# A bias table built in SBUF from SBUF by shifted row reads, and due times for ScalarE's and VectorE's work

## The chip, the cores and the metric

One core of a Trainium2 chip. The metric is the device time of one launch, in microseconds (us), as the median of several launches. Runs are compared only with runs of the kernel before on the same chip and in the fast state. Units of the profile are us unless ns is said.

## The reference, cut to what matters

```python
# q, k, v: (8 batches, 8 heads, 576 positions, 64); bias_table: (32 buckets, 8 heads)
scores = q @ k.T / 8 + bias_table[bucket(|i - j|)]     # bias depends on the distance alone, per head
x = softmax(scores) @ v                                # -> (4608 tokens, 512)
h = maximum(x @ w_in, 0.0)                             # w_in: 512 x 2048
return h * h @ w_out                                   # w_out: 2048 x 512
```

Because the bias depends only on the distance i - j, exp(bias) of one head is one row of numbers, and row p of its table is that row shifted by p. The kernel multiplies the exponentials with this table ("the band") in place of adding the bias to the scores. Beyond a certain distance the bias is constant and falls out, so the table is only 384 wide.

## The kernel before

One TensorE matmul makes the eight rows of exp(bias): `tv_sb`, 8 partitions x 512. To get the shifted copies the kernel writes them to DRAM and reads them back with overlapping rows:

```python
written = pool(tdram.ap(), tv_sb, 0.1, [tv])                 # SBUF -> DRAM, 8 KB; pool() issues on GpSimd
def table_read(h0, n):                                       # 4 heads in one DMA, row p shifted by p
    return pool(tb_sb[:, h0 : h0 + n, :],
        bass.AP(tensor=tdram, offset=512 * h0 + 1, ap=[[1, 128], [512, n], [1, 384]]), 0.3 * n, [written])
def table_mixed(e):                                          # table of the last block of keys, two heads mixed
    return pool(tm_sb[ds(64 * e, 64), :, :],
        bass.AP(tensor=tdram, offset=512 * e + 193, ap=[[1, 64], [1024, 4], [1, 192]]), 0.4, [written])
```

The work is cut into 96 units: a batch, a third of the queries (192), a pair of heads. A unit has scores `st` (TensorE), exponentials `et` (ScalarE), bands `et*tb_sb` (VectorE), products with the values `pv` (TensorE), and normalising `x_sb` (ScalarE and VectorE). Layer 1 is `hps`, layer 2 is `yps`.

Every operation goes through a planner at build time. It holds estimates (`occ`: time on the engine, `lat`: time until its result is there), advances each engine and takes from its waiting operations the one that can start first, or within a small allowance the one with the earliest due time. **What it fixes is the order of each engine's instructions. On the chip each engine then runs them in exactly that order and waits wherever a result is not there yet** (below, VectorE stands 15.39 us before one copy). An estimate that is too low therefore puts an instruction too early, and all that stands behind it on its engine waits with it.

```python
at, _, q = min((h for h in heads if h[0] <= first + wait), key=lambda h: (h[2][0].due, h[0], h[1]))
o.at, o.done = at, at + o.lat
if o.load:
    dma = max(dma, at + 1.35) + o.load
    o.done = dma + 1.15
```

## Time and profile before

| | before |
|---|---|
| median (lowest to highest) | 429.52 us (429.16 to 429.67) |
| span of the profiled run | 428.8 us |
| TensorE busy in 10-20, 20-30, 30-40 us | 9.88, 6.68, 8.05 |
| first scores, first bands, first values (`pv`), second unit's values | 9.47, 17.38, 18.28, 21.25 us |

The tenths of busy time, the stretches and the first 40 us are printed in the prediction. Two lines are added here, from the DMA view cut to the stretch from 6 to 40 us (what moves, issuing queue, count, size of one, median us from issue to landing). They are the measure for how fast the loads of keys and queries are served while the table is on its way:

```profile
kh<-in_k_dram POOLq DMA_DIRECT2D x5, 144.0 KB, 7.4
qh<-in_q_dram POOLq DMA_DIRECT2D x5, 144.0 KB, 7.5
```

### The profile page before, as it was taken

The numbers are of one execution on the slowest core, as the hardware profiler recorded it, in microseconds if no ns is written. First come the engines' busy times: TensorE is split into PE (matmuls) and PEld (weight loads), VectorE is DVE, ScalarE is ACT, GpSimd is POOL, SyncE is SP. The second block draws the span as 40 slices with busy tenths as digits, with TensorE's granted clock in tenths as the row PEclk, the third lists the DMA queues.
The fourth block names the chain that finished last, engine by engine and source line by source line (L and its number), as shares of the span: only waits on it lengthen the run. The fifth ranks groups of instructions, "written<-read, shape, count | busy, mean of one in ns | idle before, by whom it ended". The sixth has DMA issues, their size and how long they took to land.

```text
span 428.8 us, 9401 instructions
## 1 busy us (share of the span) xinstructions
PE 407.6 (95%) x3604; PEld 261.0 (61%) x3604; DVE 314.6 (73%) x939; ACT 299.1 (70%) x584; POOL 132.5 (31%) x179
## 2 busy tenths in 40 slices
PE   6968799999999998998999999999999999999996
PEld 3556587765676665665666666666666666666552
DVE  5778988757687767876867876877867876867761
ACT  2779668876888786786787787787787787784000
POOL 6874828605800192005800094004100000000000
PEclk9989999999999999999999999999999999999999
DMA  8999999959993499077991599056402300000011
GB/s 104 144 186 178 132 152 102 101 97 137 104 95 65 93 92 143 28 98 94 90 97 53 92 85 149 28 95 95 52 27 55 79 26 26 26 26 26 24 50 73
DMA packets 164717, 36.66 MB, mean 85 GB/s; under 512 B 152600, under 2 KB 159872, under 8 KB 164672
## 3 DMA queue, kind: packets, MB, share of 16 engines
q0 software_dynamic: 130048, 19.46, 58.6%
q1 hardware_dynamic: 34624, 16.60, 15.5%
q8 instruction: 28, 0.46, 0.5%
q14 instruction: 17, 0.14, 0.1%
HBM read 37.75 MB, written 16.52 MB: 127 GB/s over the span
## 4 chain that ended last, share of the span: by engine, by line
PE 81%; DVE 7%; ACT 5%; DMA 4%; issue 1%; SPq 0%; POOL 0%; POOLq 0%
PE yps L931 28%; PE hps L855 25%; PE pv L727 15%; PE st L603 7%; PE pv L701 3%; ACT et L629 3%; DMA kt<-k 2%; PE st L578 2%; DVE y L944 2%; DMA kh<-in_k_dram 1%; ACT r L769 1%; DVE x_sb L780 1%; DVE rt L874 1%; DVE et L647 1%; ACT r L799 1%
## 5 line engine op out<-in xcount | busy, mean ns | idle before, releaser
L629 ACT ACTIVATE et<-st 128x960 f16<-128x960 f32 x192 | 167.7, 882 | 60.1 <-PE st L603 59.8
L855 PE MATMUL hps<-x_sb,w_in_sb 128*128 128x384 f16 (+1 forms) x896 | 154.9, 303 | 3.2 <-DVE rt L874 1.9
L931 PE MATMUL yps<-w_out_sb,g_sb 128*128 128x512 f16 x576 | 152.0, 379 | 3.4 <-DVE y L944 2.7
L855 PEld LDWEIGHTS <-w_in_sb 128*128 128x128 f16 x896 | 83.2, 98 | 56.2 <-issue 5.6
L647 DVE TENSOR_TENSOR et<-et,tb_sb 128x384 f16<-128x384 f16 (+2 forms) x288 | 78.0, 310 | 35.6 <-ACT et L629 32.4
L234 POOL DMA_DIRECT2D vz<-in_v_dram x80 | 57.9, 743 | 135.7 <-PE pv L727 73.5
L727 PE MATMUL pv<-et,vz 128*128 128x192 f16 x804 | 86.4, 250 | 5.1 <-DVE x_sb L780 4.7
L780 DVE TENSOR_TENSOR x_sb<-pv,r 64x192 f16<-64x192 f32 x192 | 67.8, 353 | 25.8 <-ACT r L799 22.7
L931 PEld LDWEIGHTS <-g_sb 128*128 128x128 f16 x576 | 55.6, 98 | 48.7 <-issue 5.5
L727 PEld LDWEIGHTS <-vz 128*128 128x128 f16 x804 | 63.4, 99 | 20.4 <-issue 16.7
L870 DVE TENSOR_TENSOR g_sb<-rt 128x384 f16<-128x384 f16 x192 | 67.1, 355 | 5.6 <-ACT rt L866 1.4
L769 ACT ACTIVATE r<-pv 64x192 f32<-64x192 f32 x192 | 62.4, 325 | 12.3 <-PE pv L727 7.8
L866 ACT ACTIVATE rt<-hps 128x384 f16<-128x384 f32 x100 | 48.4, 486 | 27.4 <-PE hps L855 26.6
L874 DVE TENSOR_SCALAR rt<-hps 128x384 f16<-128x384 f32 x92 | 51.3, 557 | 10.9 <-PE hps L855 7.2
L603 PE MATMUL st<-qt,kt 64*128 64x192 f16 x768 | 51.3, 250 | 0.0
L234 POOL DMA_DIRECT2D k<-in_k_dram x48 | 31.0, 683 | 25.9 <-DMA q<-in_q_dram 13.6
L799 ACT ACTIVATE r<-r 128x192 f32<-128x192 f32 x96 | 34.8, 363 | 3.0
L603 PEld LDWEIGHTS <-kt 64*128 64x128 f16 x768 | 31.9, 95 | 3.6 <-issue 1.6
L944 DVE TENSOR_SCALAR y<-yps 128x512 f32<-128x512 f32 x36 | 24.8, 690 | 9.2 <-PE yps L931 8.4
L578 PEld LDWEIGHTS <-km_sb 128*128 128x128 f16 x192 | 18.6, 100 | 15.3 <-issue 0.6
L578 PE MATMUL st<-qt,km_sb 128*128 128x96 f16 x192 | 24.5, 211 | 0.1
L234 POOL DMA_DIRECT2D q<-in_q_dram x18 | 24.6, 1398 | 0.0
(32 smaller groups left out, 116.6 us busy)
## 6 DMA issues: line engine op xcount, KB each, us to landing
out_dram<-y SPq DMA_DIRECT2D x36, 256.0 KB, 2.3
vz<-in_v_dram POOLq DMA_DIRECT2D x64, 64.0 KB, 3.2
q<-in_q_dram POOLq DMA_DIRECT2D x18, 192.0 KB, 8.0
k<-in_k_dram POOLq DMA_DIRECT2D x48, 72.0 KB, 7.1
w_in_sb<-in_moe_w_in_dram POOLq DMA_DIRECT2D x4, 512.0 KB, 9.3
w_out_sb<-in_moe_w_out_dram POOLq DMA_DIRECT2D x4, 512.0 KB, 10.0
kh<-in_k_dram POOLq DMA_DIRECT2D x8, 144.0 KB, 6.7
qh<-in_q_dram POOLq DMA_DIRECT2D x8, 144.0 KB, 6.9
```

The source lines that it names most:

```text
L234: return lambda: io(eng.dma_start(out=out_, in_=in_))
L578: nc.tensor.matmul(st[:, g, 2 * IC : 2 * IC + IC // 2], km_sb[:, p % KB, :], qts[p][:, ds(c0 + g * IC // 2, IC // 2)], start=True, stop=True,)
L603: nc.tensor.matmul(st[:, e, ds(i * IC, IC)], kts[p][rows, ts(2 * g + i, 128)], qts[p][rows, ds(c0, IC)], start=True, stop=True,)
L629: io(nc.scalar.activation(out=et, in_=sts[n, g][:, :, 0:w], func=EXPF, scale=SCALE))
L647: nc.vector.tensor_tensor(out=sl, in0=sl, in1=tb_sb[:, 2 * hp : 2 * hp + 2, ds(w0, w)], op=MULT)
L727: nc.tensor.matmul(pv if jt < 4 else pv.rearrange("p (g c) -> p g c", g=2), vz[:, jt, 2 * hp + e, :], ets[n, jt // 2][:, e, ds(jt % 2 * IC ...
L769: nc.scalar.activation(out=rs[n][o : o + 64, :], in_=pvt[n, e][64 - o : 128 - o, 0:IC], func=LNF)
L780: nc.vector.tensor_tensor(out=x_sb[o : o + 64, hp, ds(ring(blk), IC)][:, ::-1], in0=pvt[n, e][o : o + 64, 0:IC], in1=rs[n][o : o + 64, :], ...
L855: nc.tensor.matmul(hps[:, ds(i * w, w)], w_in_sb[:, kk, ts(nt, 128)], x_sb[:, kk, ds(o, w)], start=(kk == 0), stop=(kk == 3),)
L870: io(nc.vector.tensor_tensor(out=g_sb[:, ts(u, k), o : o + w], in0=rt, in1=rt, op=MULT))
L874: io(nc.vector.tensor_scalar_max(out=rt, in0=hpt[blks, u][:, 0 : 2 * IC], scalar1=0.0))
L931: nc.tensor.matmul(ypt[j], g_sb[:, nt, ds(128 * m % RING, 128)], w_out_sb[:, nt, :], start=(nt == 0), stop=(nt == 15),)
```

## The change

The intent: no round trip through DRAM, fewer DMAs in GpSimd's queue, and the mixed table made by VectorE from the finished tables. Besides this the planner's load estimates are raised, and the work of ScalarE and VectorE for layer 1, transposes and key copies gets due times in place of first come, first served. The core of the diff:

```diff
-                o.done = dma + 1.15
+                o.done = dma + 1.9                        # planner: loads land later
-                0.48 * n,
+                0.6 * n,                                  # ... and take longer
-    written = pool(tdram.ap(), tv_sb, 0.1, [tv])
-    def table_read(h0, n): ...                            # 2 DMAs of 4 heads, from DRAM, GpSimd
-    def table_mixed(e): ...                               # 2 DMAs, from DRAM, GpSimd
+    def table(h):                                         # 8 DMAs of one head, from SBUF, SyncE
+        row = bass.AP(tensor=tv_sb.tensor, offset=512 * h + 1, ap=[[512, 1], [1, 128], [1, 384]])
+        return add("SP", "set", 0.45, 4.5, dma(nc.sync, tb_sb[:, h, :], row), [tv])
+    tbs = [table(h) for h in range(H)]
+    def table_mixed(e):                                   # VectorE; needs the tables of four heads
+        rows = ds(64 * e, 64)
+        src = tb_sb[rows, e::2, ds(192 - 64 * e, 192)]
+        return add("DVE", "tm", 0.4, 0.5, lambda: io(nc.vector.tensor_copy(out=tm_sb[rows, :, :], in_=src)),
+            [x[e] for x in tbs], T0 + P * 6)
...
-                [loads_qk[b, 2 * hp][w], id_in],
+                [loads_qk[b, 2 * hp][w], id_in, *(kq_ready[0] if p == 1 else [])],
...                                                        # due times: ev (transposes out of PSUM), km (key copies), turn (transposing loads)
-            r = Op("ACT", 0.41, 0.55, relu, [m, ...], LATE)
+            r = Op("ACT", 0.41, 0.55, relu, [m, ...], m.due)      # same for the two squares on VectorE
```

Note the source of each table DMA: 128 reads of 768 bytes, all from **one** partition of SBUF, each one element further. The plan counts on 4.5 us from issue to landing for every one of the eight.

> **What bounds the kernel now.** I read the page first, then busy time in stretches of 10 us, then the timeline of the first 40 us with the waits there, and last the chain of waits.
>
> ```profile
> PE   6968799999999998998999999999999999999996
> ACT  2779668876888786786787787787787787784000
> DMA  8999999959993499077991599056402300000011
> ...
> 10.00:20.00 10.00, 9.88 (x107) 5.76 (x103) 7.04 (x23) 7.01 (x9) 8.22 (x12) 1.00 0.97 135
> 20.00:30.00 10.00, 6.68 (x81) 5.28 (x81) 6.89 (x23) 7.44 (x16) 7.15 (x12) 0.84 1.34 182
> 30.00:40.00 10.00, 8.05 (x113) 6.16 (x111) 8.14 (x28) 9.71 (x19) 6.20 (x9) 0.99 1.33 200
> 40.00:50.00 10.00, 8.79 (x124) 6.66 (x123) 9.47 (x31) 8.57 (x19) 7.79 (x10) 1.00 1.24 111
> ...
> 240.00:250.00 10.00, 10.00 (x80) 6.06 (x79) 8.29 (x27) 8.12 (x18) 2.95 (x5) 1.00 0.54 96
> ```
>
> In the stretches (PE, PEld, DVE, ACT, POOL busy, then granted clock, DMA share, GB/s) TensorE is busy 10.00 of 10 us from about 100 us to 420 us, with gaps of 1 to 1.5 us only at 160-170 and 190-210. The starts of the scores (two matmuls from km_sb per unit of work, 96 units) come at 242.13 us for unit 60 and 382.30 us for unit 95: 140.17 / 35 = 4.0 us a unit, against 2.67 us of ScalarE work per unit (exponentials 1.65, two logarithms 0.67, reciprocal 0.36). So the long middle is TensorE's and no reordering on ScalarE or VectorE can shorten it much. The first 100 us are different: TensorE is busy 86 of them, some of that on warm-up matmuls that do nothing. That stage is what can be had.
>
> ```profile
> 5.61 0.68 DVE L383 CAST tv_sb<-tvp 8x512 f16<-8x512 f32 x1 [0.24 <-PE tvp L378]
> 6.58 0.54 POOL L234 DMA_DIRECT2D t_bias<-tv_sb  x1 [1.33 <-DVE tv_sb L383]
> 7.11 2.79 POOL L234 DMA_DIRECT2D vz<-in_v_dram  x4
> 8.90 0.45 PE L465 MATMUL tp<-id_sb,kh 96*64 96x96 f16 x6 [1.71 <-DMA kh<-in_k_dram]
> 9.47 0.37 PE L578 MATMUL st<-qt,km_sb 128*128 128x96 f16 x2
> 10.31 3.48 ACT L629 ACTIVATE et<-st 128x960 f16<-128x960 f32 x4 [2.54 <-PE st L603]
> 11.78 0.77 POOL L234 DMA_DIRECT2D tb_sb<-t_bias  x1 [1.89 <-DMA t_bias<-tv_sb]
> 15.29 0.80 POOL L234 DMA_DIRECT2D tb_sb<-t_bias  x1
> 17.38 2.71 DVE L647 TENSOR_TENSOR et<-et,tb_sb 128x384 f16<-128x384 f16 x12
> 18.28 1.78 PE L727 MATMUL pv<-et,vz 128*128 128x192 f16 x10
> 19.00 1.33 POOL L234 DMA_DIRECT2D tm_sb<-t_bias  x2
> 20.24 0.84 POOL L234 DMA_DIRECT2D w_in_sb<-in_moe_w_in_dram  x1
> 38.13 0.83 PE L855 MATMUL hps<-x_sb,w_in_sb 128*128 128x192 f16 x8
> ...
> tb_sb<-t_bias POOLq DMA_DIRECT2D x2, 384.0 KB, 4.9
> tm_sb<-t_bias POOLq DMA_DIRECT2D x2, 96.0 KB, 4.1
> ```
>
> The first exponential is done at about 11.3 us (10.31 + 0.98), yet the first band multiplication with the table runs at 17.38, and twelve of them come in one burst: they had piled up behind the table. The table existed in SBUF at 6.29 (5.61 + 0.68), so 11 us went into writing it to DRAM and reading it back. Values (pv) begin at 18.28. With four buffers for the exponentials, ScalarE cannot start unit 5 before that, and it idles 3.0 us in 10-20 and 2.6 us in 20-30. In 30-40 it is the bound with 9.71 busy. Layer 1 starts at 38.13, when the first block is normalised; only then has TensorE filling work.
>
> [...]GpSimd sat 1.89 us on the t_bias write, with the loads behind it in its queue. [...]the transposing load kt from SyncE lands in 2.8 us at the median, and in 6.74 us at 159 us while GpSimd's queue is full. [...]The new source rows are partitions 0 to 7. [...]I therefore take the 4.0 us per unit, not the 95%, as what TensorE needs.
>
> **The change part by part.**
>
> 1. GpSimd's queue. Five DMAs go: issue 0.54 + 0.77 + 0.80 + 1.33 = 3.44 us, and the waits 1.33 (for tv_sb) and 1.89 (for t_bias), 6.66 us in all. The loads behind start earlier: the first values at 5.25 instead of 7.11, pair 3 of keys and queries at about 9.5 instead of 13.99, the first w_in at about 13.8 instead of 20.24. Their bytes leave that queue too: 2 x 384 + 2 x 96 KB = 0.98 MB, at the 182 GB/s of 20-30 worth 5.4 us. The issue gain and the byte gain are the same gain seen twice, not a sum: loads from w_in on come some 5 to 6 us earlier if they get the engines.
>
> 2. The table itself. Eight SyncE DMAs of 96 KB, issued from about 6.3 us at 0.42 us each (SyncE's small loads take 0.40 to 0.43). [...]each lands in the 2.4 to 2.8 us of those small loads plus a little: pair 0 by about 10, all by about 14. [...]Two DVE copies are added (under 0.5 us each, VectorE 70% busy there): nothing.
>
> 3. Unit 0's scores. Pair 1's transposes now come after pair 0's evacuation, and the planner expects loads later (1.9 for 1.15, 0.6 for 0.48), which is nearer to the trace: the first kh is in use at 5.50, the old constants say 4.7, the new ones 5.7. Before, TensorE stood 1.71 us in front of pair 1's keys while pair 0 was ready (qt finished at 7.78). Scores go from 9.47 to about 7.9: 1.5 us, all of it on the path, as ScalarE waited for them.
>
> 4. Due times for layer 1's evacuation, evacuation of transposes, bands. In the middle TensorE always has work, so nothing. In 40-70, where TensorE idles 1.2 + 1.5 + 0.7 us and hps waits on rt for 1.9 us in the whole trace, earlier evacuation frees banks: about 0.5 us gained, of uncertain sign, because the same order delays exponentials on a full ScalarE.
>
> The sum on ScalarE's path: its idle time from 10 to 30 is 5.5 us, plus 1.5 us from part 3: 7.0 us if ScalarE never waited again. It will not be perfect: each unit still runs values, logarithms, reciprocal, products in a loop through two banks, and this loop takes 2.3 to 3.4 us a unit (pv at 21.25, 24.64, 26.89, 29.83, 32.48), about as long as ScalarE's own 2.67. I take 60%, 4.2 us, with part 4 inside the noise. TensorE is full afterwards, so this carries through to the end: 429.5 - 4.2 = 425.3 us.
>
> **The rivals.**
>
> A. [...]All 128 descriptors of a head read one SBUF row[...]. Then pairs 2 and 3 arrive[...] instead of about 21, VectorE (in order) stands before their bands, and values of units 5 and 6 slip from 29.83 and 32.48[...]. [...]Against it: [...]later loads are still early. It would make 428 to 433 us.
>
> B. The transfers are the bound. The DMA share is above 1 from 15 to 90 us, and 0.77 MB are only moved to the hardware queue, interleaving with the same q, k, v loads. Then only 0.2 MB are really gone and the loads for the second batch come hardly earlier. For it: shares of 1.2 to 2.0. Against it: in 10-15 the engines idled (101 GB/s) because of the bounce. It would make 426.5 to 428.
>
> C. All of the startup shifts, second batch and weights too, by the full 7 us, and the stalls at 160 and 190-210 (2.8 us) go as the order changes: 420 to 422. The stalls come from a late transposing load under a full queue, which the change does not address, so this is unlikely.
>
> **Range and chances.** I weigh the main path at 55% (424 to 426.5), A at 22%, B at 13%, C at 7%, and 3% for something worse, such as table reads blocking the engines for the q, k, v loads. That gives 425.3 us and a range of 421.8 to 430.5. Two per cent are 8.6 us: more than ScalarE's whole idle time in 10-30 with part 3, so faster by over 2% gets 0.06; slower needs the start to slip by as much, 0.04.
>
> **What the new profile would show.** Right: scores of unit 0 near 8 us, the first band before 12, first values by 13, w_in issued near 14, first hps near 31 to 34, ScalarE above 8.5 of 10 in 10-20 and 20-30, the 4.0 us per unit unchanged. Wrong in the way of A: tb_sb landing times that grow head by head[...], VectorE waiting for tb_sb. Wrong in the way of B: kh and vz landing later from issue than now, PE waiting for kh. Wrong in part 4: the spacing of units in the middle above 4.0 us, or new waits of pv for bands or of st for exponentials.

The forecast came to 429.5 - 4.2 = 425.3 us, in a range of 421.8 to 430.5. Where the text above is marked as cut, it said of the hardware what no trace or run of this case shows: how transfers wait and share, how places in SBUF are served (with a rate for such reads, and the landing times and reasons of rival A that came from it), and why the 4.0 us per unit were taken in place of the busy share. No term of the 425.3 is cut. The 428 to 433 us of A, which counted for 22% in the range, rested on the cut rate and can't be followed from what is left.

## The result, and the profile after

| | before | after |
|---|---|---|
| median (lowest to highest) of 4 runs | 429.57 (429.16 to 429.67) | 452.44 (452.05 to 453.37) |
| ratio | 1 | 1.0537, 95% interval 1.0519 to 1.0556 |

All eight runs of this table were fast. Ratios here and below are the mean time of one kernel's fast runs over the mean of the other's of the same rounds, so not quite the ratio of the medians. The verdict "same" means within 2%, "unclear" that the interval reaches across the 2% line. The change made the kernel 5.4% slower; the predicted range ended at 430.5.

The page of the kernel after: TensorE by 40 slices of 11.25 us, its granted clock, and the chain of work that ended last by engine.

```profile
PE   7415688999979999899999999999999999999996
...
PEclk9965999999999999999999999999999999999999
...
PE 70%; DVE 11%; DMA 8%; SPq 5%; ACT 2%; issue 2%; DVEq 0%
```

Where TensorE had 6, 9, 6, 8 in its first slices it now has 7, 4, 1, 5. From the eighth slice on the two rows are alike: a difference of the start that is carried to the end. SyncE's issue (SPq) and transfers (DMA) stand in the chain with 13%, where the kernel before had 4% of transfers and nothing of SyncE; the table's issues and transfers are 4% and 3% of it, the transposing loads of keys 5%. The unit starts say the same: the 60th unit starts its scores at 261.2 us (before: 242.1), the 95th at 398.2 (382.3); between them (398.2 - 261.2) / 35 = 3.9 us a unit, no slower than the 4.0 of before. At the 95th unit the new kernel is 15.9 us late and at the end of the span 21.2 (450.0 - 428.8); where the last 5.3 us come from was not looked into.

The first 40 us in stretches (busy time of PE, PEld, DVE, ACT, POOL, then granted clock, DMA share, GB/s), and the lines of the timeline that tell why:

```profile
10.00:20.00 10.00, 3.86 (x52) 2.55 (x50) 3.17 (x13) 3.00 (x4) 3.71 (x6) 1.00 1.04 61
20.00:30.00 10.00, 4.32 (x46) 2.90 (x44) 1.15 (x4) 3.54 (x6) 4.67 (x7) 0.84 1.30 119
30.00:40.00 10.00, 0.76 (x6) 0.70 (x6) 2.62 (x9) 0.00 (x0) 3.25 (x5) 0.50 1.13 151
```

```profile
6.37 22.98 SPq L233 DMA_DIRECT2D tb_sb<-tv_sb  x8
...
18.03 1.16 DVE L649 TENSOR_TENSOR et<-et,tb_sb 128x384 f16<-128x384 f16 x5 [6.43 <-DMA tb_sb<-tv_sb]
...
36.54 0.35 DVE L401 COPY tm_sb<-tb_sb 64x768 f16<-64x768 f16 x1 [15.39 <-DMA tb_sb<-tv_sb]
...
39.24 1.76 PE L729 MATMUL pv<-et,vz 128*128 128x192 f16 x10 [14.91 <-DVE x_sb L782]
```

Read the last block from the top. The eight issues keep SyncE 22.98 us (0.56 to 5.5 us each), where 8 x 0.42 = 3.4 us had been counted on: it looks as if SyncE is held while earlier transfers are undone, which was not shown. The first bands run at 18.03 after a wait of 6.43. At 36.54 comes the key line: VectorE's next instruction is the copy into the mixed table, it needs the seventh table, and VectorE stands before it for 15.39 us. The normalising of unit 0 (`x_sb`) stands behind it on VectorE, so the second unit's `pv` on TensorE wait 14.91 us, ScalarE has nothing to do (0.00 in 30-40), and the granted clock shows 0.50 in the same stretch, in which TensorE is busy 0.76 of 10 us.

The same DMA view of 6 to 40 us as shown of before:

```profile
tb_sb<-tv_sb SPq DMA_DIRECT2D x8, 96.0 KB, 13.8
kh<-in_k_dram POOLq DMA_DIRECT2D x5, 144.0 KB, 14.4
qh<-in_q_dram POOLq DMA_DIRECT2D x5, 144.0 KB, 14.3
```

The tables take 13.8 us at the median, and loads that have nothing to do with them land after 14.4 us in place of 7.4. Two suspects, then: the tables are late and stand in front of VectorE, or the slow reads slow everything else.

### The profile page after: what moved, and what is told of

The parts are those of the page before. It is cut to its first block, busy times and chain, and to the rows that moved or that the text cites. A ratio compares the mean times of both kernels' runs of the same rounds, so it can differ in the third digit from the quotient of the medians.

```text
span 450.0 us, 9425 instructions
## 1 busy us (share of the span) xinstructions
PE 410.2 (91%) x3615; PEld 262.8 (58%) x3615; DVE 316.1 (70%) x946; ACT 298.4 (66%) x579; POOL 129.1 (29%) x174
## 3 DMA queue, kind: packets, MB, share of 16 engines
q1 hardware_dynamic: 35776, 17.38, 18.4%
## 4 chain that ended last, share of the span: by engine, by line
PE 70%; DVE 11%; DMA 8%; SPq 5%; ACT 2%; issue 2%; DVEq 0%
PE yps L933 24%; PE hps L857 22%; PE pv L729 13%; PE st L605 5%; DMA kt<-k 5%; SPq L233 4%; DMA tb_sb<-tv_sb 3%; PE pv L703 3%; DVE x_sb L782 2%; DVE rt L876 2%; DVE et L649 2%; PE st L580 2%; DVE g_sb L872 2%; DVE y L946 1%; SPq L532 1%
## 5 line engine op out<-in xcount | busy, mean ns | idle before, releaser
L857 PE MATMUL hps<-x_sb,w_in_sb 128*128 128x384 f16 (+1 forms) x896 | 152.3, 303 | 3.3 <-DVE rt L876 1.6
L933 PE MATMUL yps<-w_out_sb,g_sb 128*128 128x512 f16 x576 | 149.6, 379 | 3.6 <-DVE y L946 3.4
L782 DVE TENSOR_TENSOR x_sb<-pv,r 64x192 f16<-64x192 f32 x192 | 67.8, 353 | 24.9 <-ACT r L801 21.7
L868 ACT ACTIVATE rt<-hps 128x384 f16<-128x384 f32 x95 | 46.2, 487 | 33.9 <-PE hps L857 33.7
L876 DVE TENSOR_SCALAR rt<-hps 128x384 f16<-128x384 f32 x97 | 54.0, 557 | 11.1 <-PE hps L857 7.1
```

The source lines that it names most:

```text
L782: nc.vector.tensor_tensor(out=x_sb[o : o + 64, hp, ds(ring(blk), IC)][:, ::-1], in0=pvt[n, e][o : o + 64, 0:IC], in1=rs[n][o : o + 64, :], ...
L857: nc.tensor.matmul(hps[:, ds(i * w, w)], w_in_sb[:, kk, ts(nt, 128)], x_sb[:, kk, ds(o, w)], start=(kk == 0), stop=(kk == 3),)
L876: io(nc.vector.tensor_scalar_max(out=rt, in0=hpt[blks, u][:, 0 : 2 * IC], scalar1=0.0))
L933: nc.tensor.matmul(ypt[j], g_sb[:, nt, ds(128 * m % RING, 128)], w_out_sb[:, nt, :], start=(nt == 0), stop=(nt == 15),)
```

## The experiments

My theory was the place of the source: all reads of one table come from one partition and are served one after the other, so are those of neighbouring partitions, and the eight heads follow each other. The rivals: that many reads of one row, or SBUF to SBUF transfers as such, are slow; that the transfers in general were the bound; and that the due times or the new estimates did the damage. Where the expectations speak of this theory by a letter, it is A. Each expectation was on record before its run.

### 1. The transfer by itself

The kernel before, with transfers of 96 KB appended in the quiet tail, each kind waiting for the one before (one look, its state unknown, 536.47 us as planned by the addition; the result stays right). Not shown in the cut are a first read of the row and one of the row without the shift; this last did not wait for the read before it.

```diff
+    io(nc.sync.dma_start(out=pr["row"], in_=row(0)))              # one row, shifted
+    io(nc.sync.dma_start(out=pr["across"], in_=g_sb[:, 0, 0:384]))  # source over 128 partitions
+    io(nc.sync.dma_start(out=pr["dram"], in_=bass.AP(tensor=tdram, offset=1, ap=[[1, 128], [1, 384]])))
+    for h in range(H): io(nc.sync.dma_start(out=pr8[:, h, :], in_=row(h)))     # eight heads
+    for to, other in ((same, 1), (apart, 4)):                     # two queues, 4 + 4
+        for i in range(4):
+            io(nc.sync.dma_start(out=to[0][:, i, :], in_=row(0)))
+            io(nc.scalar.dma_start(out=to[1][:, i, :], in_=row(other)))
```

> The kernel before, with table-sized transfers (128 rows of 768 B) issued one at a time after its last output, when no other transfer runs. Theory A[...]: one head from one row takes 4 us or more[...], the same rows without the shift too, the copy whose source is spread over 128 partitions about 2 us, the rows read from DRAM about 2 to 3 us; eight heads in a row about 29 us. Two queues at once: four heads of partition 0 and four of partition 1[...] 29 us, four of partition 0 and four of partition 4[...] clearly less, 15 to 20. Theory B (the transfers are only slow because the load queue competes for the engines): one head about 2.5 us, eight about 8, no difference between sources. Theory C (one row is what is slow[...]): like A, but partitions 0 and 1 together as fast as 0 and 4.

The timeline of the tail (start, duration, and in brackets what VectorE's copy waited for, so the time of the transfer):

```profile
436.95 0.14 DVE L1024 COPY tv_sb<-pr_row 8x1 f16<-8x1 f16 x1 [5.93 <-DMA pr_row<-tv_sb]
...
442.33 0.14 DVE L1024 COPY tv_sb<-pr_across 8x1 f16<-8x1 f16 x1 [2.08 <-DMA pr_across<-g_sb]
...
447.01 20.81 SPq L1039 DMA_DIRECT2D pr_eight<-tv_sb  x8
477.61 0.14 DVE L1024 COPY tv_sb<-pr_eight 8x1 f16<-8x1 f16 x1 [30.57 <-DMA pr_eight<-tv_sb]
...
511.73 0.14 DVE L1024 COPY tv_sb<-pr_same 8x1 f16<-8x1 f16 x1 [32.58 <-DMA pr_same<-tv_sb]
...
532.17 0.14 DVE L1024 COPY tv_sb<-pr_apart 8x1 f16<-8x1 f16 x1 [18.91 <-DMA pr_apart<-tv_sb]
```

The same 96 KB land in 5.4 us (the first read) and 5.9 us from one row and in 2.0 us from 128 partitions; with the row in DRAM it took 2.9. Eight heads in a row take 30.6 us, 3.8 us a head: 98,304 B / 3.8 us = 26 GB/s. The same row read without the shift landed 8.4 us after issue, but it was queued behind another row read; from the landing of that one it took 3.1 us, so leaving out the shift does not bring it to the 2.0 of the spread source. The 29 us expected of eight heads can be had as an estimate from the kernel after: there pairs 0, 1 and 2 landed at 17.9, 25.1 and 32.9 us, 3.6 to 3.9 us a head, and 8 x 3.6 = 29. Two queues with sources on partitions 0 and 1 gain nothing (32.6 us for eight transfers); with sources on partitions 0 and 4 the same eight take 18.9. So it is neither the SBUF to SBUF transfer as such (2.0 us from 128 partitions) nor that single rows are read (18.9 us against 32.6): it counts on which partitions the rows lie. By what means was not shown. The long issue goes with it: SyncE was held 20.81 us by the eight issues here too, with nothing else running.

### 2. The table undone, and the table alone

Kernel after with the table of before; and kernel before with the table of after (both are the table hunk of the diff above, taken back and put in).

> The changed kernel with the table of before (through DRAM on GpSimd's queue), all other parts of the change kept. If the slow table is the whole loss: 427 to 430 us, since unit 0's scores come some 0.6 us earlier as in the changed kernel. If the new due times or the new transfer estimates cost something: above 433.

> The kernel before with the table part of the change alone. If the slow table is the loss: 445 to 455 us, with tb_sb landing after 7 to 17 us and VectorE held for over 10 us on tb_sb. If the loss needs the new due times: below 435.

Measured: 430.95 us without the new table (ratio 1.0017, 0.9984 to 1.005), 454.63 us with the table alone (1.0572, 1.0532 to 1.0613). The whole loss is the table's. The due times and estimates without it give nothing that can be told from zero.

### 3. The same eight transfers, with the rows in DRAM

Everything of the change stays, SyncE's eight DMAs and VectorE's copies too. Only the rows are written to DRAM first and read from there:

```diff
+    written = add("SP", "set", 0.45, 2.6, dma(nc.sync, tdram.ap(), tv_sb), [tv])
-        row = bass.AP(tensor=tv_sb.tensor, offset=512 * h + 1, ap=[[512, 1], [1, 128], [1, 384]])
+        row = bass.AP(tensor=tdram, offset=512 * h + 1, ap=[[1, 128], [1, 384]])
```

> The changed kernel, with one edit: SyncE first writes the eight rows to DRAM, and the same eight transfers read them there. Same queue, same sizes, same order. Theory A: transfers land in 3 to 5 us, all by about 16 us, VectorE does not wait for tb_sb, and the start is as I had predicted: 423 to 427 us. Theory B (competition with the loads on the same engines): landing times stay above 8 us and the time above 440.

Measured: 432.99 us (1.0058, 1.0018 to 1.0099). The timeline of this kernel:

```profile
10.52 5.07 SPq L234 DMA_DIRECT2D tb_sb<-t_bias  x8
...
16.70 2.45 DVE L652 TENSOR_TENSOR et<-et,tb_sb 128x384 f16<-128x384 f16 x10 [3.18 <-DMA tb_sb<-t_bias]
17.21 1.77 PE L732 MATMUL pv<-et,vz 128*128 128x192 f16 x10 [2.62 <-DMA vz<-in_v_dram]
```

The eight issues take 5.07 us in place of 22.98, the tables land 4.9 to 6.5 us after issue. Some 19 of the 23 us are back (452.4 - 433.0, from two chips; against before, 0.6% are left of 5.4%) with the rows in DRAM as the source: here the detour through DRAM beats the direct way. The start is now about 1 us ahead of before (first values at 17.21 in place of 18.28, where they wait 2.62 us for a load), and yet the kernel is 0.6% slower than before: that lead is lost later.

### 4. The planner told of the late tables

One-row reads as in the kernel after, but with its landing times put into the plan, so that VectorE's copy is not put too early. The figures do not all stand at their own head: by the trace, heads 0 to 7 took 6.6, 10.9, 15.3, 15.4, 17.2, 13.6, 13.3 and 14.0 us, so the plan has head 2 some 4 us too early and head 6 some 4 us too late. The same plan is used once more in section 10.

```diff
-        return add("SP", "set", 0.45, 4.5, dma(nc.sync, tb_sb[:, h, :], row), [tv])
+        occ = (0.56, 0.6, 2.1, 5.0, 4.6, 3.9, 0.6, 5.5)[h]
+        lat = (6.6, 9.7, 10.9, 15.3, 15.4, 16.3, 17.2, 13.1)[h]
+        return add("SP", "set", occ, lat, dma(nc.sync, tb_sb[:, h, :], row), [tv])
```

> The changed kernel; only the planner's figures for the eight table transfers are set to what the trace showed (issue 0.56 to 5.5 us, landing 6.6 to 17.2 us), so it places the two mixed-table copies and the bands where the tables are there. The transfers stay as slow. If the standing of VectorE in front of the mixed-table copy is most of the loss of 22 us: 433 to 440 us. If it is the slow transfers themselves, with the loads they hold up: above 445.

Measured: 449.10 us (1.0442, 1.038 to 1.0504). The long wait before the copy is gone, and only about a per cent with it. What TensorE then waited for, in 8 to 60 us (waits: us in total, times, longest):

```profile
PE tp L468 <- DMA kh<-in_k_dram: 7.9, 2, 4.5
```

The keys themselves now come late: `kh` landed 14.1 us after issue in 6 to 40 us. So a new wait had taken the old one's place, and I could not yet say which of the two was *the* loss.

### 5. The planner's new estimates alone

```diff
-                o.done = dma + 1.15
+                o.done = dma + 1.9
-                0.48 * n,
+                0.6 * n,
-                [loads_qk[b, 2 * hp][w], id_in],
+                [loads_qk[b, 2 * hp][w], id_in, *(kq_ready[0] if p == 1 else [])],
```

> The kernel before with part 3 alone: the planner's new load figures and pair 1's transposes after pair 0's evacuation; old table, old due times. My prediction said 1.5 us earlier scores carried to the end: 428. If the start is set by the loads and not by ScalarE: 429 to 431, the 0.6 to 1 us lost by the end.

Measured: 433.67 us (1.0091, 1.0024 to 1.0159): a loss of nearly a per cent (verdict: same; two of its runs took 431.4 and 431.8 us, two 435.6 and 435.9, and why is not known), where I had counted 1.5 us of gain on unit 0's scores. Unit 0's scores do start earlier (8.88 us, before 9.47), but nothing of it is left in the end.

### 6. The round trip kept, but on SyncE's queue

Kernel before; the write to DRAM and the eight reads from there on SyncE, the mixed table by VectorE's copies. No estimates or due times changed. Run again later in five rounds.

```diff
-    written = pool(tdram.ap(), tv_sb, 0.1, [tv])
+    written = add("SP", "set", 0.45, 4.4, dma(nc.sync, tdram.ap(), tv_sb), [tv])
+    def table(h):
+        row = bass.AP(tensor=tdram, offset=512 * h + 1, ap=[[1, 128], [1, 384]])
+        return add("SP", "set", 0.45, 5.5, dma(nc.sync, tb_sb[:, h, :], row), [written])
```

> The kernel before with one edit: the table goes through DRAM as before but on SyncE's queue (one write, eight reads, planned with the times that the earlier run showed: 4.4 and 5.5 us), the mixed table by two VectorE copies; GpSimd's queue is free of it. If GpSimd's queue was a bound of the start, as part 1 of the prediction has it: 425 to 428. If the transfers as such are (rival B): 428 to 432.

> The SyncE bounce again, with more rounds, to see whether its 428.9 us against 429.2 is a gain: between 0.990 and 1.002 of the kernel before.

Measured: 428.93 us (0.9984, 0.9935 to 1.0033), and again 429.29 us (0.9998, 0.9962 to 1.0034). GpSimd's queue is relieved of the table as the change intended, the first `w_in_sb` is issued at 14.29 and 14.73 us in place of 20.24, and the time is the same. That part of the expected gain is worth nothing here. Nor is the first `pv` a measure of the end in this range: they start at 21.81 in the second of these runs, 3.5 us later than before, and the time does not show it.

### 7. Two more attempts at a faster version

Run 3's kernel with measured table times in the plan and the transposing loads' due times as before; and run 6's kernel with two reads of four heads in place of eight reads.

```diff
-            add("SP", "turn", 1.25, 3.4, dmat(*x), halves[b] + [s_last.get(p - KB)], T0 + P * (first_use[p] - 2))
+            add("SP", "turn", 1.25, 3.4, dmat(*x), halves[b] + [s_last.get(p - KB)])
```

```diff
-        row = bass.AP(tensor=tdram, offset=512 * h + 1, ap=[[1, 128], [1, 384]])
+        rows = bass.AP(tensor=tdram, offset=512 * h0 + 1, ap=[[1, 128], [512, 4], [1, 384]])
```

> The run with rows from DRAM (433.0 us), with its planner told the measured times and with one part of the change taken back: the transposing loads are due at once again, not two units before their use. In that run the lead of 1.3 us of TensorE work at 100 us was gone at 120. If the later due time of these loads costs it: 427 to 430. If not: 431 to 434.

> The SyncE bounce with two reads of four heads instead of eight of one: fewer issues, the same bytes and rows. Expected equal to the eight: 427 to 430 us; below 426 it would be the best version.

Measured: 430.81 us (1.0021, 0.9976 to 1.0066) and 428.46 us (0.9966, 0.9919 to 1.0013). Neither is told from before. No version of this study clearly beats it.

### 8. Does a slow row read slow a load beside it?

In the quiet tail again: a load like that of the keys, issued from GpSimd, alone and then beside four SyncE transfers of each kind (one look, its state unknown).

```diff
+        for i in range(0 if n == "nothing" else 4):
+            io(nc.sync.dma_start(out=st4[n][:, i, :], in_=src))     # src: 128 partitions, DRAM rows, one SBUF row
+        io(nc.gpsimd.dma_start(out=ld[n], in_=k[0, 0:2].rearrange("h (p t) d -> p h (t d)", t=TPP)))
```

> The kernel before, and in its quiet tail one load of keys by GpSimd's queue (two heads, 96 rows of 1536 B each, cast to half the size), four times: with nothing beside it, beside four table-sized SyncE transfers whose source is spread over 128 partitions, beside four that read shifted rows in DRAM, beside four that read one SBUF row. If the one-row reads hold the engines up for others: alone about 3 to 4 us, beside the spread and the DRAM sources at most twice that, beside the one-row reads 10 us or more, ending nearly when they end (about 15 us). If the engines serve both queues fairly: beside one-row reads no more than beside the DRAM rows.

```profile
441.91 0.15 DVE L1040 COPY end_dram<-ld_dram 96x1 f16<-96x1 f16 x1 [6.61 <-DMA ld_dram<-in_k_dram]
...
443.31 0.63 POOL L1034 DMA_DIRECT2D ld_row<-in_k_dram  x1 [7.21 <-DVE end_row L1039]
450.16 0.15 DVE L1040 COPY end_row<-ld_row 96x1 f16<-96x1 f16 x1 [7.02 <-DMA ld_row<-in_k_dram]
...
459.89 0.16 DVE L1042 COPY end_row<-by_row 128x1 f16<-128x1 f16 x1 [2.84 <-DMA by_row<-tv_sb]
```

From issue to landing the load took 3.1 us alone, 3.8 beside sources spread over 128 partitions, 6.3 beside DRAM rows and 6.8 beside one-row reads (443.31 to 450.16, where the copy runs that waits for it). I had expected 10 us or more in the last case and missed: the load is slowed to about twice, but is not held until the row reads are through at 459.89. DRAM rows slow a load nearly as much; the comparison is not quite even, as they were issued 3.0 us before their load (432.45 and 435.48), the row reads 0.2 us before theirs. What differs is how long it goes on: the four one-row reads are under way from 443.10 to 459.89, 16.8 us, where the four of DRAM rows landed within 7.1 us of their issue. Loads that follow meet the row reads too.

### 9. Two heads only from the SBUF row

Run 6's kernel, heads 0 and 1 straight from SBUF, the other six through DRAM.

```diff
+        if h < 2:
+            row = bass.AP(tensor=tv_sb.tensor, offset=512 * h + 1, ap=[[512, 1], [1, 128], [1, 384]])
```

> The SyncE bounce (428.9 us) with the first two of eight heads read straight from their SBUF rows, as in the change, and six through DRAM. If the loss is the time in which one-row reads hold the engines (3.8 us a head, 21 us for eight): a quarter of it, 433 to 436 us. If it were mostly VectorE standing before late tables or a matter of order: 427 to 430, since unit 0's table is then early.

Measured: 430.67 us (1.0027, 0.9982 to 1.0071), a miss: the loss is not a quarter of 23 us. The two heads are there at 16.34 us, 9.6 us after the first issue, and the first bands run only at 20.81. It would fit that the length of the series costs; this run does not show it.

### 10. Late, or slowing others?

These last three were run to settle what runs 2 to 4 had left open. First the changed kernel with its eight rows on partitions 0, 4, ..., 28 in place of 0 to 7, so that no two lie closer than the 0 and 4 of run 1 (18.9 us, against 32.6 for 0 and 1):

```diff
-    tv_sb = single.tile([H, 512], FP16, name="tv_sb")
+    tv_sb = single.tile([4 * H, 512], FP16, name="tv_sb")       # the matmul writes row 4h for head h
-        row = bass.AP(tensor=tv_sb.tensor, offset=512 * h + 1, ap=[[512, 1], [1, 128], [1, 384]])
+        row = bass.AP(tensor=tv_sb.tensor, offset=512 * 4 * h + 1, ap=[[512, 1], [1, 128], [1, 384]])
```

Second, the changed kernel with its order of work untouched, but the tables come from DRAM and each pair of heads is issued only when the pair before has landed: late as after (fourth head at 24.9 and seventh at 37.5 us, after: 25.1 and 36.5), yet without reads of one row. Third, the same with the plan of run 4, which knows of the lateness.

```diff
+            if h in (2, 4, 6):   # reads a corner of the two tables before: SyncE waits here until they have landed
+                io(nc.sync.dma_start(out=late_sb[:, 2 * h : 2 * h + 2], in_=tb_sb[0:1, h - 2 : h, 0]))
-        row = bass.AP(tensor=tv_sb.tensor, offset=512 * h + 1, ap=[[512, 1], [1, 128], [1, 384]])
+        row = bass.AP(tensor=tdram, offset=512 * h + 1, ap=[[1, 128], [1, 384]])
```

> The changed kernel with the eight source rows on partitions 0, 4, ..., 28[...] in place of 0 to 7[...]. If one transfer still reads one row[...] and the transfers of the one SyncE queue go one after the other, nothing changes: 3.6 to 3.8 us a head, last table at 35 to 38 us, 449 to 454 us in all. If the 16 engines run ahead into the next transfers of the queue[...]: last table before 25 us, 430 to 442 us. I hold the first for likelier (65%).

> The changed kernel, its order of work unchanged, but the tables come from DRAM, each pair of heads issued only once the pair before has landed: late, by some 6 us a pair (about 16, 22, 28 and 33 us)[...]. If the lateness of the tables is the loss (engines in order standing before them): 445 us or more, key loads in the first 40 us landing in about 8 us. If the loss is that slow reads slow the key, query and value loads: 433 to 440 us.

> As the run before, with the planner told the late landing times of the tables as in the run that told it of them (449.1 us with one-row reads). The tables late as there, the reads not slow to others. If slowed loads make the loss of that run: 430 to 437 us. If lateness makes it: 445 us or more.

Measured: 440.38 us with the rows four partitions apart (1.0242, 1.0188 to 1.0296); 456.66 us late from DRAM (1.0605, 1.0545 to 1.0665); 439.80 us late from DRAM and told (1.0221, 1.0175 to 1.0267). The first and the last are slower than before, but whether by over 2% is unclear.

The kernel with the rows apart, whose mixed-table copy and second unit of values answer to the 36.54 and 39.24 of after:

```profile
25.64 0.35 DVE L402 COPY tm_sb<-tb_sb 64x768 f16<-64x768 f16 x1 [8.71 <-issue]
...
28.87 1.76 PE L730 MATMUL pv<-et,vz 128*128 128x192 f16 x10 [8.62 <-DVE x_sb L783]
```

I held "no change" for likelier, and it fell: with nothing altered but the partitions of the source (and, to fill them, one memset and a wider small matmul), tables 0 to 6 are there by 25.6 us in place of 36.5, and half of the loss is gone. So the place of the source rows counts inside the kernel too. From the first issue at 6.3 us the seven tables took 19.3 us, 2.8 each, where the series of run 1 took 3.8: it would fit transfers of one queue that overlap in part when their rows lie apart. That, and what limits it, was not shown.

The kernel with late tables from DRAM, its order that of after:

```profile
37.63 0.35 DVE L413 COPY tm_sb<-tb_sb 64x768 f16<-64x768 f16 x1 [18.31 <-DMA tb_sb<-t_bias]
...
40.04 1.76 PE L741 MATMUL pv<-et,vz 128*128 128x192 f16 x10 [17.84 <-DVE x_sb L794]
```

It stands before the same copy as the kernel after, 18.31 us long, with no one-row reads at all; its `kh` landed after 9.4 us (after: 14.4). So lateness together with that order is enough for the whole loss (it lost 4 us more than after; what these are I did not find out). Set the untold kernels in a row by the start of the second unit's values: run 3 at 20.17 us, rows apart at 28.87, after at 39.24, late from DRAM at 40.04. Their times are 433.0, 440.4, 452.4 and 456.7. From the first to the third, 19.1 us of later values are 19.4 us of longer time: nearly one for one.

Told of the lateness, the two kernels part. With row reads (run 4) TensorE waited 7.9 us for keys; with late DRAM reads the list of TensorE's waits in the same stretch begins as follows, and there are no keys in it:

```profile
PE pv L743 <- DVE x_sb L796: 2.6, 4, 1.3
PE st L594 <- ACT et L645: 2.6, 2, 1.7
```

Its tables are as late as run 4's (fourth head 24.5 against 24.7 us, seventh 37.9 against 36.1), but its `kh` landed after 8.7 us where run 4's took 14.1. 1.0442 against 1.0221 is 2.2% or some 9.5 us: the price of slowed loads once the order is mended.

## Why the prediction was wrong

By its own steps:

1. **GpSimd's queue**: the issue gain came (values issued at 5.19 us, pair 3's keys at 9.38), but not the gain from it. In after the same queue then waits for slowed loads (2.71, 1.04, 1.69 and 1.12 us for values), and the first `w_in_sb` goes out at 20.27, no earlier than before. Where the table is not in the way (run 6: 14.73) the earlier loads are worth 0.0 to 0.2% (1.0 less the ratios of its two runs), inside their intervals. The step's arithmetic held; that it lies on the path did not.

2. **The table: this step failed.** Beside "pair 0 by about 10, all by about 14" it worked out a second case, one head after the other (cut, as its rate came from no run of this case), and then built the sum on the first. The series is what happened: 3.8 us a head by itself, and in the kernel pair 0 at 17.9, pair 1 at 25.1, pair 2 at 32.9 and pair 3 at 37.9 us. The comparison with SyncE's small loads (2.4 to 2.8 us) was not one of like with like: those read DRAM, these all read one partition of SBUF. The step also put "two DVE copies ... nothing". They are 0.35 us each, but they need seven and eight of the eight tables, and the plan had put them where 4.5 us of landing would have made them ready. Their own time was right, their place in an in-order engine cost 15.39 us of waiting.

3. **Unit 0's scores**: they came earlier by 0.7 us (8.81 for 9.47), and in run 3 by 1.6 us (7.91), about as predicted, but the estimates alone (run 5) lost 0.9%. A gain of that size at 9 us was not on the path that sets the end. I can show where one such lead went: counting the columns of all matmuls of scores, values and layers off the traces, run 2's kernel with the old table had 17.1% of the work done at 100 us (before 16.5%), and at 140 it had 26.8% (26.9%). In between VectorE waited twice, 1.9 us in all, for keys of the second batch from the transposing loads (before: not at all). That this is the cause is argued, not shown; changing those loads' due times (run 7) could not be told from before.

4. **Due times**: nothing, as predicted in the middle: units stay at 3.9 to 4.0 us.

Two readings were off without deciding anything. Of the 11 us that "went into writing it to DRAM and reading it back" the first half of the table took 9.3: it was there at 15.62 us, and VectorE was busy with transposes and key copies until the bands at 17.38. And 2 x 384 KB are 0.79 MB by the count that made 0.98 MB of 960 KB, not 0.77 (the pages show 16.60 MB in q1 hardware_dynamic before, 17.38 after: 0.78 more).

Of the **rivals**, A had the series of tables that come late from single rows, and was given 22% and "428 to 433 us". It was mis-sized by 20 us, as it let only the values of units 5 and 6 slip. In fact all after unit 0 slipped to 39, since the mixed copy stood in front. The 3% for "table reads blocking the engines for the q, k, v loads" were real too, as loads at half speed and not as blocking. Putting the ratios in a row (the steps depend on each other; the ratios are from different chips, each against before on its own): tables from DRAM in time and told 1.0021 (run 7, which also has the old due times of the transposing loads); the same late 1.0221; the same with row reads 1.0442; the same untold, the kernel after, 1.0537. So about 2.0% for lateness, 2.2% for slowed loads, 1.0% for the order, each uncertain by 0.6 to 0.8 (from the intervals). The last two stand in for each other: mend the order alone, and the kernel waits for keys (run 4, 1.0442); take away the slow reads alone but leave the tables late, and it waits before the copy (1.0605, more than the whole loss).

**B**, that transfers are the bound, has more in it than 13%: run 3 with the table repaired still had its first values wait 2.62 us for a load, and no version was clearly faster. **C** fell.

## What to carry to other kernels

Before you make copies of one SBUF row by DMA, look at the partitions of the source, not only at the bytes, and measure the transfer by itself: here a row in SBUF served 26 GB/s (3.8 us a head in series), the detour through DRAM was faster (433.0 us against 452.4), and rows four partitions apart took back half of the loss (440.4). A small instruction that needs the last of a series of transfers is a barrier on an engine that runs in order (15.39 us here); place it by a measured landing time, or late (here that alone got back about 1%, as the next wait took over). When the case of a series has been worked out and only an argument by likeness speaks against it, a range that does not include it carried to the end of the chain is too narrow (430.5 at the top, 452.4 measured).
